# Attention with one low part of k for two heads, reciprocals as 64-column blocks, and split-weight memory in three tiles

## The chip, the cores and the metric

The kernel runs on one core of a Trainium2 chip. The metric is the device time of one execution in microseconds, the median of several runs. The profile is one further execution taken by the hardware profiler. Five engines work from queues of their own: TensorE (PE; its weight loads are shown as PEld), VectorE (DVE), ScalarE (ACT), GpSimd (POOL) and SyncE (SP), which here only issues DMA transfers. Each queue is worked off in order, and an instruction waits at its queue's head until its semaphores are there.

## The reference

Three steps follow one another: attention with pooled queries, a squared-ReLU MLP and an expert layer in which each token goes to one expert.

```python
q_pool = q.reshape(B, H, S // 2, 2, D).mean(axis=3)             # B, H, S, D = 2, 8, 1152, 64
scores = np.matmul(q_pool, k.transpose(0, 1, 3, 2)) / np.sqrt(D)
attn = np.exp(scores - scores.max(-1, keepdims=True))
attn = attn / (attn.sum(-1, keepdims=True) + 1e-09)
x = np.matmul(attn, v)                                          # then (B * S/2, H * D) = (1152, 512)
h = np.maximum(x @ w_in, 0.0)                                   # 512 -> 2048 -> 512
x = (h * h) @ w_out
# top-1 experts: softmax of x @ w_gate, argmax, at most `capacity` tokens per expert,
# out[i] = gate[i] * (relu(x[i] @ w1[e]) @ w2[e]),  8 experts, 512 -> 1024 -> 512
```

## The kernel before, in words

**Attention** works on 8 pairs of heads (a batch and two heads each). A pair has 9 tiles of 128 query rows: for each head four full tiles, and one tail tile in which the 64 last rows of both heads stand together. `tiles` (line 253) lists them: after the first pair always head 0 and head 1 of one row block in turn. For accuracy each fp32 operand of a score is split into a high part that the fast fp32r matmul takes exactly and a low rest. `kqs` holds k and q of a head twice, in partitions 0 to 63 and 64 to 127. `q_piece` (296) has ACT scale the high part of q, `q_low` (301) has DVE put the low part of q into the lower half of the same tile `qT`, and POOL copy the tail's columns into `qzs`. `k_piece` (313) makes, in thirds of 384 columns, the high part of k (line 318 on ACT or 320 on POOL) and its low part `kl` (321, POOL except in the first pair), each head in a set of its own, `kts`; there are four sets, for two pairs of heads. In `s_unit` (326) a third of a full tile's scores takes two matmuls: `qT` with the high k (337, this gives high times high and low times high at once) and `qT` with `kl` (339), whose second half is zero. The tail's third takes four, two per head.

A step of the loop (`run_step`, 432) is, in order: score thirds 0 and 1 of tile n, a transposition group of an older tile (`t_unit`, 363), what a burst held up, third 2, the maximum (`s_max`, DVE, 344), another transposition group, the exponential (`s_exp`, ACT, 349, which also sums), the copy of the first group (380), then, in some steps, a burst; then the extras, the middle transposition group with its copy on DVE (379), and `s_rec` (354): the reciprocal of tile n-1's sums, one column. Scores lie in two sets of PSUM banks that alternate; the third transposition group of an older tile uses the rest of the same banks. The middle group (`TG`, 361) has blocks 4 to 6 of the exponentials and, as fourth, the reciprocal broadcast to 128 columns, so that a transposition puts it along the free axis. A `burst` (383) multiplies the transposed blocks of four tiles with v: 18 matmuls per head pair on PE, then DVE multiplies each head's half with its reciprocal (403, two operations), ACT makes the high part `xh` (407) and POOL the low part `xl` (408). The second burst of a pair, in the next pair's fourth step, is followed by one for the tail. `at(n, ...)` hangs extras on steps; the calls around line 507 hang the preparation of pair p+1 on the steps of pair p: for the second head the sum of q at step 5 of the pair (from 0), piece 0 of k and `q_piece` at 6, `q_low` and piece 1 at 7, piece 2 at 8; in the first pair all one step later.

**Memory of the split weights.** One fp32r tile `ar` (78) holds `xh` and `xl`, and behind them a region that is used twice: in attention for `kts` and `qzs`, then for 16 slots of 1024 columns, which the ring `slots` (192) gives to the high and low halves of the MLP weights, and for the halves of g. `split_hi` and `split_lo` (195, 203) fill two slots, `drop` (213) gives them back. The expert stage takes the whole tile anew as `ar2` (920), so that its loads wait until all of it has fallen free.

**MLP** (`g1`, 751, and `g2`, 776): 48 items of 384 tokens by 128 hidden columns; `mat(n, f, front)` hangs work on item n, before or behind its `g2`. Expert weights, 64 units of 512 KB, are loaded through SP's queue (`load_experts`, 742) into whatever `stage` has free, two thirds through the MLP into another tile, `af`.

**Experts.** Routing of the last tokens, three scatters of token rows by POOL (`scatter`, 557), then `load_disp` (954) reads the rows of each expert back; it waits for the scatters. The first 64 rows of expert 0 come by matmuls (`gather`, 693) instead. `run_batch` (1150) goes through experts 0 to 3, then `rest` (1097) through what they have beyond 64 rows, then 4 to 7.

```python
for o in range(room[0], R0 + RW - UW + 1, UW):     # line 1120
    stage.give(ar2[:, o : o + UW])
load_experts(4)
for e in range(NDT):
    load_disp(e, (0,))
load_experts()
```

Of the kernel before, what the change touches and what calls it, by code (L numbers as in the profile page):

```python
# [9 lines left out]
F32 = mybir.dt.float32  # L10
# [11 lines left out]
def tile_pooled_attention__relu2_mlp__top1_experts(  # L22
# [54 lines left out]
    RW = max(NSET * SETW + 4 * P, NSLOTB * UW + 2 * GB * TB)  # L77
    ar = keep.tile([P, R0 + RW], F32R, name="ar", tag="ar")
# [12 lines left out]
    xh = ar[:, :XN].rearrange("p (a n) -> p a n", a=NPAIR)  # L91
    xl = ar[:, XN : 2 * XN].rearrange("p (a n) -> p a n", a=NPAIR)
# [99 lines left out]
    slots = Ring([ar[:, R0 + i % NSLOTB * UW : R0 + (i % NSLOTB + 1) * UW] for i in range(NSLOTB - 4, 2 * NSLOTB - 4)])  # L192
# [28 lines left out]
    NSET = 4  # L221
# [4 lines left out]
    def kt_set(i):  # L226
        o = R0 + i * SETW
        return ar[:, o : o + S], ar[:, o + S : o + 2 * S], ar[:, o + 2 * S : o + SETW]

    kts = [kt_set(i) for i in range(NSET)]  # L230
    qzs = [
        ar[:, R0 + NSET * SETW + i * 2 * P : R0 + NSET * SETW + (i + 1) * 2 * P].rearrange("p (h n) -> p h n", h=2)
        for i in range(2)
    ]
# [30 lines left out]
    def bufs_of(p, h):  # L265
        return kts[p % 2 * 2 + h]

# [28 lines left out]
    def q_piece(p, h, c=slice(0, SQ)):  # L296
        qT = bufs_of(p, h)[2]
        src = kqs[h][:, S : S + SQ][:, c]
        nc.scalar.activation(out=qT[:, c], in_=src, func=AF.Copy, scale=QSCALE)

    def q_low(p, h, c=slice(0, SQ)):
        qT = bufs_of(p, h)[2]
# [10 lines left out]
    def k_piece(p, h, i, eng=None, hi=None):  # L313
        kh, kl, _ = bufs_of(p, h)
# [6 lines left out]
        (eng or (nc.gpsimd if p else nc.vector)).tensor_tensor(out=kl[:D, c], in0=src[:D], in1=kh[:D, c].bitcast(F32), op=ALU.subtract)  # L321
# [4 lines left out]
    def s_unit(n, i):  # L326
# [4 lines left out]
        c = slice(KS * i, KS * (i + 1))  # L331
        if h is None:
            ops = [(h, qzs[p % 2][:, h, :]) for h in range(2)]
        else:
            ops = [(h, bufs_of(p, h)[2][:, j * P : (j + 1) * P])]
        for m, (h, lhs) in enumerate(ops):
            nc.tensor.matmul(ps, lhsT=lhs, rhs=bufs_of(p, h)[0][:, c], start=(m == 0), stop=False)  # L337
        for m, (h, lhs) in enumerate(ops):
            nc.tensor.matmul(ps, lhsT=lhs, rhs=bufs_of(p, h)[1][:, c], start=False, stop=(m == len(ops) - 1))  # L339


    def s_max(n):
        nm = st[n]["nm"] = sm.tile([P, 1], F32, tag="nm", name="nm", bufs=4)
        nc.vector.tensor_reduce(out=nm, in_=st[n]["S"][:, :, :KS], axis=AX.XY, op=ALU.max, negate=True)  # L344

    def s_exp(n):
        pr = st[n]["P"] = prs[n % NPB]
        su = st[n]["sum"] = sm.tile([P, 1], F32, tag="su", name="su", bufs=4)
# [4 lines left out]

    def s_rec(n):
        su = st[n]["sum"]
        rc = st[n]["rc"] = sm.tile([P, 1], F32, tag="rc", name="rc", bufs=4)
        nc.vector.tensor_scalar(out=su, in0=su, scalar1=1e-9, scalar2=None, op0=ALU.add)
        nc.vector.reciprocal(out=rc, in_=su)


    TG = (range(4), (4, 5, 6, None), (7, 8))

    def t_unit(n, i):
# [4 lines left out]
        else:  # L368
            src = bank_sets[(n + LAG[2]) % 2][:, :2, KS:]
        for m, c in enumerate(TG[i]):  # L370
            x = st[n]["rc"].to_broadcast([P, P]) if c is None else st[n]["P"][:, c * P : (c + 1) * P]
            nc.tensor.transpose(src[:, m, :], x, ident)  # L372
        blocks = slice(4 * i, 4 * i + len(TG[i]))
# [9 lines left out]
    def burst(p, u):  # L383
# [102 lines left out]
    for i in range(NSET):  # L486
        (nc.vector if i == 0 else nc.gpsimd).memset(kts[i][1][D:].bitcast(F32), 0.0)
    for z in qzs:
        nc.gpsimd.memset(z.bitcast(F32), 0.0)
# [17 lines left out]
    for p in range(NPR - 1):  # L507
        n0 = NT9 * p
        for h in range(2):
# [5 lines left out]
            for i in (1, 2):  # L515
                at(m + 1 + i, lambda p=p, h=h, i=i: k_piece(p + 1, h, i, hi=nc.gpsimd))
# [8 lines left out]
    for w in range(5):  # L525
# [5 lines left out]
        n = (when[3 * w + 2] + 2, 0, 64, 67, N + 1)[w] or when[3 * w + 2] + 2  # L531
# [17 lines left out]
    ghs = Turn([ar[:, R0 + NSLOTB * UW + i * TB : R0 + NSLOTB * UW + (i + 1) * TB] for i in range(GB)])  # L549
    gls = Turn([ar[:, R0 + NSLOTB * UW + (GB + i) * TB : R0 + NSLOTB * UW + (GB + i + 1) * TB] for i in range(GB)])  # L550
# [290 lines left out]
    mat(PB + 2 * FH + 1, make_sel)  # L841
    for tb in range(NTB - 1):
# [19 lines left out]
    for n in range(NI):  # L862
# [5 lines left out]
        for f in mtodo.pop((n, 2), []):  # L868
            f()
# [16 lines left out]
    g2(*items[-1], (2,))  # L886
    logits_b(lt + 0, lb[0])
# [32 lines left out]
    ar2 = keep.tile([P, R0 + RW], F32, name="ar2", tag="ar")  # L920
# [199 lines left out]
    for o in range(room[0], R0 + RW - UW + 1, UW):  # L1120
        stage.give(ar2[:, o : o + UW])
    load_experts(4)
# [106 lines left out]
```

## Time and profile before

| | us |
|---|---|
| median of 3 runs (lowest to highest) | 644.79 (644.01 to 646.36) |
| profiled execution, its own time | 646.28 |
| its span, first to last instruction | 644.6 |
| PE busy, weight loads busy | 602.3, 465.2 |
| DVE, ACT, POOL busy | 356.3, 257.2, 162.6 |

Durations below are those of the profiled execution. An engine's busy time is the time in which at least one of its instructions runs. A PE instruction is pipelined: its own duration is longer than the distance to the next one. A timeline row has the start, the duration, the engine, the line of the kernel, the operation, what it writes and reads (in the program's tile names) and how many equal ones were merged; in brackets stands the engine's idle time before it and what ended it. A row that groups instructions has their count, the busy time, the mean duration of one in ns, and the idle time before them.

### The profile page before, as it was taken

Reading aid. Unit: us, or ns where it says so; the run is one execution under the profiler, and the core shown is the slowest. Engines: PE = TensorE matmul, PEld = TensorE weight load, DVE = VectorE, ACT = ScalarE, POOL = GpSimd, SP = SyncE. Lnnn points to the kernel's source line nnn. Section 1 sums busy time; section 2 is a strip of 40 time slices with the busy share of each in tenths; the row PEclk is TensorE's granted clock in tenths of the full one; section 3 lists DMA queues with packets and bytes.
Section 4 is the critical chain, followed back from the end, with each engine's and each line's share of the span. In section 5 each row is a group of like instructions: output and inputs, shape, how many; then the busy total and the mean of one; then the engine's idle time right before and its main releaser. Section 6 shows DMA issues by size and latency. Waiting matters only on the chain. (4 is left out here: it accounts for less than half of the span.)

```text
span 644.6 us, 10110 instructions
## 1 busy us (share of the span) xinstructions
PE 602.3 (93%) x3873; PEld 465.2 (72%) x3873; DVE 356.3 (55%) x655; ACT 257.2 (40%) x511; POOL 162.6 (25%) x223
## 2 busy tenths in 40 slices
PE   5889999999999999999999999999999798999994
PEld 2667787878787878788999999989888344444342
DVE  4777878787878777758467894233545010201110
ACT  3656666666666666632323233232433111110010
POOL 3152636181616263210001330001002301000011
PEclk9999999999999999999999999999999989999998
DMA  8496683353353301303133387001000696399900
GB/s 215 113 317 198 191 255 93 111 140 92 94 156 95 105 36 39 130 13 118 54 104 117 122 293 294 1 0 39 3 2 18 224 397 175 105 393 353 310 9 13
DMA packets 35994, 89.23 MB, mean 138 GB/s; under 512 B 4257, under 2 KB 5157, under 8 KB 35936
## 3 DMA queue, kind: packets, MB, share of 16 engines
q1 hardware_dynamic: 34240, 85.07, 41.9%
q0 software_dynamic: 1376, 2.81, 1.2%
q8 instruction: 35, 0.57, 0.4%
q10 hardware_dynamic: 320, 0.59, 0.3%
q14 instruction: 23, 0.19, 0.1%
HBM read 78.55 MB, written 11.37 MB: 139 GB/s over the span
## 5 line engine op out<-in xcount | busy, mean ns | idle before, releaser
L759 PE MATMUL bs<-ar 128*128 128x384 f32 x576 | 109.0, 338 | 0.0
L759 PEld LDWEIGHTS bs<-ar 128*128 128x128 f32 x576 | 101.7, 188 | 4.7 <-issue 1.2
L344 DVE TENSOR_REDUCE nm<-sc 128x1 f32<-128x1152 f32 x72 | 97.5, 1354 | 10.1 <-PE sc L339 9.0
L337 PE MATMUL sc<-ar 128*128 128x384 f32 x240 | 91.5, 397 | 12.0 <-ACT ar L318 5.4
L349 ACT ACTIVATE af<-sc,nm 128x1152 f32<-128x1152 f32 x72 | 88.0, 1222 | 31.8 <-DVE nm L344 30.3
L785 PE MATMUL bt<-ar 128*128 128x512 f32 x360 | 93.0, 395 | 1.2 <-DVE ar L771 1.2
L339 PE MATMUL sc<-ar 128*128 128x384 f32 x240 | 79.4, 347 | 0.6 <-POOL ar L321 0.6
L785 PEld LDWEIGHTS bt<-ar 128*128 128x128 f32 x360 | 66.4, 188 | 13.8 <-DVE ar L771 1.6
L765 ACT ACTIVATE af<-bs 128x384 f32<-128x384 f32 x48 | 23.6, 491 | 121.6 <-PE bs L759 112.3
L769 DVE TENSOR_TENSOR af<-af 128x384 f32<-128x384 f32 x48 | 28.4, 591 | 72.3 <-ACT af L765 72.3
L397 PE MATMUL ba<-af 128*64 128x256 f32 x576 | 65.7, 382 | 0.6 <-DVE af L379 0.6
L337 PEld LDWEIGHTS sc<-ar 128*128 128x128 f32 x240 | 45.3, 194 | 22.6 <-ACT ar L318 8.5
L379 DVE COPY af<-ba 128x512 f32<-128x512 f32 x72 | 49.3, 685 | 14.5 <-PE ba L372 14.3
L397 PEld LDWEIGHTS ba<-af 128*64 128x64 f32 x576 | 39.9, 137 | 21.8 <-issue 2.3
L380 ACT ACTIVATE af<-bm 128x512 f32<-128x512 f32 x72 | 43.0, 597 | 25.5 <-PE bm L372 25.5
L339 PEld LDWEIGHTS sc<-ar 128*128 128x128 f32 x240 | 46.3, 194 | 2.0 <-POOL ar L321 1.1
L408 POOL TENSOR_TENSOR ar<-af,ar 128x256 fp32r<-128x256 f32 (+1 forms) x24 | 13.9, 593 | 125.8 <-ACT ar L407 125.8
L372 PE MATMUL bm<-ident,af 128*128 128x128 f32 x288 | 43.7, 275 | 0.7 <-ACT af L380 0.6
L201 POOL TENSOR_SCALAR ar<-af 128x1024 fp32r<-128x1024 f32 x15 | 21.2, 1414 | 89.2 <-DVE af L175 54.7
L321 POOL TENSOR_TENSOR ar<-af,ar 64x384 fp32r<-64x384 f32 x42 | 41.9, 998 | 3.5
L372 PE MATMUL ba<-ident,af 128*128 128x128 f32 x216 | 36.6, 278 | 4.6 <-DVE af L379 4.3
L372 PEld LDWEIGHTS bm<-ident,af 128*128 128x128 f32 x288 | 36.1, 142 | 3.8 <-ACT af L380 1.4
(186 smaller groups left out, 799.8 us busy)
## 6 DMA issues: line engine op xcount, KB each, us to landing
af<-in_moe_w_dram SPq DMA_DIRECT2D x32, 512.0 KB, 8.7
ar<-in_moe_w_dram SPq DMA_DIRECT2D x32, 512.0 KB, 9.9
af<-in_q_dram SPq DMA_DIRECT2D x30, 288.0 KB, 3.6
af<-in_k_dram SPq DMA_DIRECT2D x29, 288.0 KB, 5.6
af<-in_moe_w_in_dram SPq DMA_DIRECT2D x8, 1024.0 KB, 6.7
af<-in_moe_w_out_dram SPq DMA_DIRECT2D x8, 1024.0 KB, 4.9
disp<-af SPq DMA_DIRECT2D x6, 771.0 KB
af<-in_v_dram SPq DMA_DIRECT2D x8, 576.0 KB, 4.5
```

What stands on the lines that cost most here:

```text
L321: (eng or (nc.gpsimd if p else nc.vector)).tensor_tensor(out=kl[:D, c], in0=src[:D], in1=kh[:D, c].bitcast(F32), op=ALU.subtract)
L337: nc.tensor.matmul(ps, lhsT=lhs, rhs=bufs_of(p, h)[0][:, c], start=(m == 0), stop=False)
L339: nc.tensor.matmul(ps, lhsT=lhs, rhs=bufs_of(p, h)[1][:, c], start=False, stop=(m == len(ops) - 1))
L344: nc.vector.tensor_reduce(out=nm, in_=st[n]["S"][:, :, :KS], axis=AX.XY, op=ALU.max, negate=True)
L349: nc.scalar.activation(out=pr.rearrange("p (i s) -> p i s", i=3), in_=st[n]["S"][:, :, :KS], func=AF.Exp, bias=st[n]["nm"], accum_out=su,)
L372: nc.tensor.transpose(src[:, m, :], x, ident)
L379: return lambda: nc.vector.tensor_copy(out=dst, in_=src)
L380: return lambda: nc.scalar.activation(out=dst, in_=src, func=AF.Copy)
L397: nc.tensor.matmul(wide(av[hrows[h]]), lhsT=vs[:, h, c * D : (c + 1) * D], rhs=of(c + (c >= RB), h), start=(c == 0), stop=(c == NKC - 1),)
L759: nc.tensor.matmul(ph[:, :TB], lhsT=w[:, cw], rhs=x[:, d, tb * TB : (tb + 1) * TB], start=(n == 0), stop=(n == 3 * NDC - 1),)
L769: nc.vector.tensor_tensor(out=g, in0=r, in1=r, op=ALU.mult)
L785: nc.tensor.matmul(accs[tb][t], lhsT=g[:, ct], rhs=w[:, cw], start=(f == 0 and n == 0), stop=(f == FH - 1 and n == 2),)
```

## The change

The low part of k of both heads now lies in one tile, head 0 in partitions 0 to 63, head 1 in 64 to 127. Each head gets a second scaled copy of q, `q2s`, that is zero in the other head's partitions; the low matmul takes it instead of `qT`. A tail third takes three matmuls, since `qz2` with the shared `kl` serves both heads. `s_rec` writes the reciprocal 64 times, head 0 in the left half and head 1 in the right half of a block; only head 1's tile (and the tail) transposes it, and a full burst needs one multiplication. The region behind `xh` and `xl` becomes three tiles of 6, 6 and 4 slots; the first two hold a pair's k and q in attention. `regrow(i)` takes tile i anew for expert weights: the first at MLP item 46, the second after the last `g2`, the third where the expert weights were loaded before. The rows of experts are read before those, expert 1 first. The fifth split runs at step 72 instead of 73.

```diff
+    GROUPS = (6, 6, 4)
+    ax = keep.tile([P, R0 + 2 * GB * TB], F32R, name="ax", tag="ax")
+    gr_ = [keep.tile([P, n * UW], F32R, name=f"gs{i}", tag=f"gs{i}") for i, n in enumerate(GROUPS)]
...
+    slots = Ring([v for i in (2, 0, 1) for v in cut(gr_[i])])
...
     def q_piece(p, h, c=slice(0, SQ)):
...
-        nc.scalar.activation(out=qT[:, c], in_=src, func=AF.Copy, scale=QSCALE)
+        own = halves_of[h]
+        nc.scalar.activation(out=qts[h][:, c], in_=src, func=AF.Copy, scale=QSCALE)
+        nc.scalar.activation(out=q2s[h][own, c], in_=src[own], func=AF.Copy, scale=QSCALE)
...
         if c.stop == SQ:
-            nc.gpsimd.tensor_scalar(
-                out=qzs[p % 2][:, h, h * D : h * D + TAIL], in0=qT[:, NF * P :].bitcast(F32),
-                scalar1=1.0, scalar2=0.0, op0=ALU.mult, op1=ALU.add,
-            )
+            for o, x in ((qz[:, h, hc], qT[:, NF * P :]), (qz2[own, hc], q2s[h][own, NF * P :])):
+                nc.gpsimd.tensor_scalar(
+                    out=o, in0=x.bitcast(F32), scalar1=1.0, scalar2=0.0, op0=ALU.mult, op1=ALU.add
+                )
...
-        (eng or (nc.gpsimd if p else nc.vector)).tensor_tensor(out=kl[:D, c], in0=src[:D], in1=kh[:D, c].bitcast(F32), op=ALU.subtract)
+        (nc.gpsimd if p else nc.vector).tensor_tensor(
+            out=kl[own, c], in0=src[own], in1=kh[own, c].bitcast(F32), op=ALU.subtract
+        )
...
         if h is None:
-            ops = [(h, qzs[p % 2][:, h, :]) for h in range(2)]
+            ops = [(qz[:, h, :], khs[h]) for h in range(2)] + [(qz2, kl)]
         else:
-            ops = [(h, bufs_of(p, h)[2][:, j * P : (j + 1) * P])]
-        for m, (h, lhs) in enumerate(ops):
-            nc.tensor.matmul(ps, lhsT=lhs, rhs=bufs_of(p, h)[0][:, c], start=(m == 0), stop=False)
-        for m, (h, lhs) in enumerate(ops):
-            nc.tensor.matmul(ps, lhsT=lhs, rhs=bufs_of(p, h)[1][:, c], start=False, stop=(m == len(ops) - 1))
+            jc = slice(j * P, (j + 1) * P)
+            ops = [(qts[h][:, jc], khs[h]), (q2s[h][:, jc], kl)]
+        for m, (lhs, rhs) in enumerate(ops):
+            nc.tensor.matmul(ps, lhsT=lhs, rhs=rhs[:, c], start=(m == 0), stop=(m == len(ops) - 1))
...
     def s_rec(n):
...
-        rc = st[n]["rc"] = sm.tile([P, 1], F32, tag="rc", name="rc", bufs=4)
+        if h is None:
+            rc = st[n]["rc"] = sm.tile([P, 1], F32, tag="rt", name="rt")
+        else:
+            if h == 0:
+                rcs[z] = sm.tile([P, P], F32, tag="rc", name="rc")
+            st[n]["rc"] = rcs[z]
+            rc = rcs[z][:, h * D : (h + 1) * D]
         nc.vector.tensor_scalar(out=su, in0=su, scalar1=1e-9, scalar2=None, op0=ALU.add)
-        nc.vector.reciprocal(out=rc, in_=su)
+        nc.vector.reciprocal(out=rc, in_=su.to_broadcast(rc.shape))
-    TG = (range(4), (4, 5, 6, None), (7, 8))
+    TG = (range(4), (4, 5, 6), (7, 8))
...
+        if i == 1 and h != 0:
+            nc.tensor.transpose(src[:, nb, :], st[n]["rc"].to_broadcast([P, P]), ident)
+            nb += 1
...
-        for h in range(2):
-            nc.vector.tensor_tensor(
-                out=wide(x[hrows[h]]), in0=wide(av[hrows[h]]), in1=of(RB, h, hrows[h]), op=ALU.mult
-            )
+        if u < 2:
+            nc.vector.tensor_tensor(out=wide(x), in0=wide(av), in1=of(RB, 1), op=ALU.mult)
+        for h in range(2 if u == 2 else 0):
+            nc.vector.tensor_tensor(out=x[hrows[h]], in0=av[hrows[h]], in1=of(RB, h, hrows[h]), op=ALU.mult)
...
-                at(m + 1 + i, lambda p=p, h=h, i=i: k_piece(p + 1, h, i, hi=nc.gpsimd))
+                at(min(m + 1 + i, n0 + NT9 - 1), lambda p=p, h=h, i=i: k_piece(p + 1, h, i, hi=nc.gpsimd))
...
-        n = (when[3 * w + 2] + 2, 0, 64, 67, N + 1)[w] or when[3 * w + 2] + 2
+        n = (when[3 * w + 2] + 2, 0, 64, 67, 72)[w] or when[3 * w + 2] + 2
...
+    def regrow(i):
+        t = keep.tile([P, GROUPS[i] * UW], F32, name=f"gf{i}", tag=f"gs{i}")
+        for v in cut(t):
+            stage.give(v)
+        load_experts()
+
+    mat(2 * PB - 2, lambda: regrow(0), 3)
...
     g2(*items[-1], (2,))
+    regrow(1)
...
-    for o in range(room[0], R0 + RW - UW + 1, UW):
-        stage.give(ar2[:, o : o + UW])
-    load_experts(4)
-    for e in range(NDT):
+    for e in (1, 0, *range(2, NDT)):
         load_disp(e, (0,))
-    load_experts()
+    for v in cut(ar2[:, room[0] :]):
+        stage.give(v)
+    regrow(2)
```

## Rows read from the trace of the kernel before

**Rows 1.** Busy time by stage (length, then each engine's busy time, granted clock, DMA).

```profile
0.00:275.00 275.00, 254.22 (x2000) 208.46 (x2000) 206.88 (x373) 172.47 (x334) 118.97 (x162) 1.00 0.49 140
275.00:497.00 222.00, 220.32 (x1220) 196.87 (x1221) 127.11 (x218) 67.09 (x135) 24.91 (x26) 1.00 0.24 85
```

**Rows 2.** Timeline, one tile between two bursts, sixth pair: PE, DVE, ACT.

```profile
177.17 0.41 PE L337 MATMUL sc<-ar 128*128 128x384 f32 x1 [0.20 <-ACT af L380]
...
178.78 1.36 DVE L344 TENSOR_REDUCE nm<-sc 128x1 f32<-128x1152 f32 x1 [0.33 <-PE sc L339]
...
180.18 1.22 ACT L349 ACTIVATE af<-sc,nm 128x1152 f32<-128x1152 f32 x1 [0.43 <-DVE nm L344]
...
181.39 0.37 ACT L380 ACTIVATE af<-sc 128x256 f32<-128x256 f32 x1
```

**Rows 3.** Timeline behind the second burst of a pair: DVE, then PE.

```profile
193.23 0.69 DVE L379 COPY af<-ba 128x512 f32<-128x512 f32 x1
...
194.23 1.34 DVE L344 TENSOR_REDUCE nm<-sc 128x1 f32<-128x1152 f32 x1
...
197.30 0.44 PE L337 MATMUL sc<-ar 128*128 128x384 f32 x1 [0.42 <-ACT af L380]
```

**Rows 4.** Timeline at the border of two pairs: PE in tail and next tile, POOL.

```profile
171.36 0.52 PE L339 MATMUL sc<-ar 128*128 128x384 f32 x2
171.72 0.52 PE L337 MATMUL sc<-ar 128*128 128x384 f32 x2
...
172.51 0.72 POOL L408 TENSOR_TENSOR ar<-af,ar 128x256 fp32r<-128x256 f32 x1 [5.18 <-ACT ar L407]
173.21 0.23 POOL L308 TENSOR_SCALAR ar<-ar 128x64 fp32r<-128x64 f32 x1
...
175.56 1.00 POOL L321 TENSOR_TENSOR ar<-af,ar 64x384 fp32r<-64x384 f32 x1
...
175.76 0.34 PE L339 MATMUL sc<-ar 128*128 128x384 f32 x1
```

**Rows 5.** Timeline, start of the expert stage: SP's loads, PE.

```profile
499.76 1.76 SPq L740 DMA_DIRECT2D ar<-in_moe_w_dram  x4
...
512.49 0.60 PE L971 MATMUL ba<-ident,af 64*128 64x64 f32 x4 [3.31 <-DMA af<-disp]
...
513.57 6.57 PE L994 MATMUL bs<-af,ar 128*64 128x512 f32 x16 [0.47 <-ACT ar L975]
...
521.84 3.65 PE L994 MATMUL bs<-ar 128*64 128x512 f32 x16
```

**Rows 6.** Busy time in two microseconds of that stretch, columns as in rows 1.

```profile
514.00:516.00 2.00, 2.00 (x6) 0.48 (x4) 0.00 (x0) 0.00 (x0) 0.17 (x1) 0.50 0.91 285
```

**Rows 7.** Groups by line and shape: count, busy us, mean ns, idle before.

```profile
L403 DVE TENSOR_TENSOR af<-ba,af 64x256 f32<-64x256 f32 x32 | 13.5, 422 | 26.7 <-PE ba L397 26.2
...
L358 DVE RECIPROCAL rc<-su 128x1 f32<-128x1 f32 x72 | 11.8, 164 | 2.5
...
L299 ACT ACTIVATE ar<-af 128x576 fp32r<-128x576 f32 x15 | 10.1, 675 | 0.9 <-POOL af L294 0.9
...
L372 PEld LDWEIGHTS ba<-ident,rc 128*128 128x128 f32 x72 | 9.8, 136 | 0.7
...
L403 DVE TENSOR_TENSOR af<-bm,af 64x64 f32<-64x64 f32 x16 | 3.6, 223 | 1.5 <-PE bm L397 1.2 <-issue 0.2
...
L713 DVE RECIPROCAL af<-rse 128x3 f32<-128x3 f32 x3 | 0.5, 177 | 0.0
```

**Rows 8.** Timeline at the border of the first two pairs: PE.

```profile
44.99 0.34 PE L339 MATMUL sc<-ar 128*128 128x384 f32 x1
...
48.92 0.45 PE L339 MATMUL sc<-ar 128*128 128x384 f32 x1 [0.63 <-POOL ar L321]
```

**Rows 9.** Line 558's scatters, from issue to landing: from 440 to 490, then from 498 to 505.

```profile
DMA to landing us min/median/max: 2.9/3.3/3.6
...
DMA to landing us min/median/max: 6.3/6.8/7.0
```

More of the change, by code (lines that the diff above doesn't have):

```diff
@@ L76, in tile_pooled_attention__relu2_mlp__top1_experts @@
     NSLOTB = 16
-    RW = max(NSET * SETW + 4 * P, NSLOTB * UW + 2 * GB * TB)
-    ar = keep.tile([P, R0 + RW], F32R, name="ar", tag="ar")
+    GROUPS = (6, 6, 4)
+    ax = keep.tile([P, R0 + 2 * GB * TB], F32R, name="ax", tag="ax")
+    gr_ = [keep.tile([P, n * UW], F32R, name=f"gs{i}", tag=f"gs{i}") for i, n in enumerate(GROUPS)]
+    assert sum(GROUPS) == NSLOTB and 2 * SETW + 2 * P <= 6 * UW
     widths = dict(kq=4 * S, pr=3 * S, pt=6 * (S + P), vs=2 * NKC * D, xr=2 * P + D)
@@ L190, in tile_pooled_attention__relu2_mlp__top1_experts, with cut @@
     nwork = [narrow_ops(kind, g, u == 6) for u, (kind, g) in enumerate(units)]
-    slots = Ring([ar[:, R0 + i % NSLOTB * UW : R0 + (i % NSLOTB + 1) * UW] for i in range(NSLOTB - 4, 2 * NSLOTB - 4)])
+    def cut(t):
+        return [t[:, i * UW : (i + 1) * UW] for i in range(t.shape[-1] // UW)]
+    slots = Ring([v for i in (2, 0, 1) for v in cut(gr_[i])])
     halves = {}
@@ L220, in tile_pooled_attention__relu2_mlp__top1_experts @@
     KS = S // 3
-    NSET = 4
     att = ExitStack()
@@ L224, in tile_pooled_attention__relu2_mlp__top1_experts, with pair_set @@
     bank_sets = [pool.tile([P, 3, 512], F32, name=f"sc{i}") for i in range(2)]
[L226 to L234, printed above, removed]
+    ZW = 3 * P
+    PW = 3 * S + 4 * SQ + ZW
+    def pair_set(i):
+        x = gr_[i][:, :PW]
+        khs = [x[:, h * S : (h + 1) * S] for h in range(2)]
+        kl, q0 = x[:, 2 * S : 3 * S], 3 * S
+        qts = [x[:, q0 + h * SQ : q0 + (h + 1) * SQ] for h in range(2)]
+        q2s = [x[:, q0 + (2 + h) * SQ : q0 + (3 + h) * SQ] for h in range(2)]
+        z = x[:, q0 + 4 * SQ :]
+        return khs, kl, qts, q2s, z[:, : 2 * P].rearrange("p (h n) -> p h n", h=2), z[:, 2 * P :]
+    psets = [pair_set(i) for i in range(2)]
+    halves_of = (slice(0, D), slice(D, 2 * D))
     vs = part("vs", 0, 2 * NKC * D).rearrange("p (h r) -> p h r", h=2)
@@ L347, in s_exp @@
         pr = st[n]["P"] = prs[n % NPB]
-        su = st[n]["sum"] = sm.tile([P, 1], F32, tag="su", name="su", bufs=4)
+        su = st[n]["sum"] = sm.tile([P, 1], F32, tag="su", name="su", bufs=3)
         nc.scalar.activation(
@@ L485, in tile_pooled_attention__relu2_mlp__top1_experts @@
     nc.gpsimd.memset(warm, 0.0)
[L486 to L489, printed above, removed]
+    nc.vector.memset(psets[0][1][D:].bitcast(F32), 0.0)
+    for i in range(2):
+        for h in range(2):
+            (nc.vector if i + h == 0 else nc.gpsimd).memset(psets[i][3][h][halves_of[1 - h]].bitcast(F32), 0.0)
+        for z in psets[i][4:]:
+            nc.gpsimd.memset(z.bitcast(F32), 0.0)
     for _ in range(WARM):
@@ L548, in tile_pooled_attention__relu2_mlp__top1_experts @@
     xts = Turn([af[:, K0 + i * XTW : K0 + (i + 1) * XTW] for i in range(2)])
-    ghs = Turn([ar[:, R0 + NSLOTB * UW + i * TB : R0 + NSLOTB * UW + (i + 1) * TB] for i in range(GB)])
-    gls = Turn([ar[:, R0 + NSLOTB * UW + (GB + i) * TB : R0 + NSLOTB * UW + (GB + i + 1) * TB] for i in range(GB)])
+    ghs = Turn([ax[:, R0 + i * TB : R0 + (i + 1) * TB] for i in range(GB)])
+    gls = Turn([ax[:, R0 + (GB + i) * TB : R0 + (GB + i + 1) * TB] for i in range(GB)])
     hbank = Turn(bank_s)
@@ L867, in tile_pooled_attention__relu2_mlp__top1_experts @@
             g2(*items[n - 2])
-        for f in mtodo.pop((n, 2), []):
-            f()
+        for x in (2, 3):
+            for f in mtodo.pop((n, x), []):
+                f()
     for key in sorted(mtodo):
```

30 lines of the change are left out of this document (17 added, 13 removed).

## The prediction

> **What bounds the kernel now.** I read the windows by stage first, then the timeline of one steady pair of heads, then the waits around the start of the expert stage. The windows [rows 1] show that PE is busy for 254 of the 275 us of attention and for 220.3 of the 222 us of the MLP; DVE, the next, has 207 and 127. In the MLP nothing but PE counts. In attention the busy share misleads, because a ring stands behind it. Call the nine tiles of a pair k0 to k8 (k8 is the tail tile of both heads); the burst (value product) of the first four stands in k7's step, that of the rest in the next pair's k3. In [rows 2] the score matmuls of a tile start at 177.17, DVE takes the maximum at 178.78, ACT the exponential at 180.18 and a copy at 181.39 that ends at 181.76, and only then is the score bank free for the tile two later; the first row says that PE had idled 0.20 for just such a copy. From the start of the maximum to PE's next use of the bank are 3.0 us, whatever PE does meanwhile. Behind a pair's second burst DVE feeds this ring late [rows 3]: the copy at 193.23 and the maximum at 194.23 are one unbroken DVE queue with the sum and reciprocal between them, and PE's tile at 197.30 comes 3.07 after that maximum, with 0.42 idle before it. At the border between two pairs PE runs without a gap [rows 4]: there, work taken from PE is time. In the expert stage PE idles 3.31 us for the rows of expert 1 [rows 5], and then runs 16 matmuls in 6.57 us that take 3.65 us a little later; the granted clock is 0.50 in that stretch, 1.2 instead of 2.4 GHz [rows 6].
>
> **The change part by part.** *Tail tile.* A third of its scores takes 3 matmuls instead of 4. Four matmuls start in 0.72 us, two in 0.36 (171.36 to 171.72 [rows 4]), so 0.18 each, 0.54 per pair. The reciprocal's transpose of one first-head tile in that step goes too: bounded by nothing and by its weight load of 136 ns [rows 7], I take 0.1. PE would reach the last low matmul of the next pair's k0 at 175.76 - 0.64 = 175.12 [rows 4].
>
> *Low k shared by the heads.* The matmul of k0 with kl now reads the rows of both heads, so k0 waits for the second head's three pieces as well. POOL makes the last two of them, and its queue is in order: they stand behind the burst's write-back at 172.51, which waits for ACT, and the last ends at 175.56 + 1.00 = 176.56 [rows 4]. Before, only k1 needed it. The write-back comes earlier by one multiplication of 422 ns [rows 7], and one more copy like that at 173.21 adds 0.23: 176.37. PE therefore idles about 1.3 us in k0 and does its last low matmul 0.6 later than now. Nothing is queued on PE that could pass it: k0's maximum and k1's matmuls stand behind. Between that matmul and k1 lie eight transposes, and k1 used to idle 0.20 there; k1 starts 0.64 later less this idle time, 0.2 to 0.45, I take 0.3; and through the ring so does k3, whose step holds the burst. The 0.54 gained is thus swallowed. Six borders: +1.8. At the first border POOL is later still: k0's last low matmul stands at 44.99, the wait for POOL in k1 ends at 48.92 [rows 8]. After the change k0 waits until about 48.5 (0.42 earlier), and k1 comes a full tile behind, 1.1 later at 49.6. Its maximum follows after 1.61 (177.17 to 178.78 [rows 2]) and k3 after 3.07 more, at 54.3; now the chain from 48.92 with a matmul of 0.45 gives 52.5. That is 1.8. After the last tail no pair follows: -0.5. Sum of the borders: +3.1.
>
> *Reciprocal over 64 columns.* 64 tiles write 64 copies of a reciprocal instead of one. No row shows that. One element takes 164 ns, three take 177 [rows 7], 6.5 ns an element; 63 more make +0.41. From below, an ordinary 64 by 64 operation takes 223, which would be +0.06; below that nothing speaks for a gain, since the output only grows. From above, with 2 ns of scatter on the difference, 7.5 ns an element or +0.47. I take 0.41, the row of the same operation. The Trainium skill ("VectorE: DVE Perf Modes", First, the fixed hardware budget) says that a reciprocal iterates a divide with a repeat count of 8 and gives the clock as 0.96 GHz; worked out from that, an estimate, 63 elements cost 0.53, and the sum below would be 0.9 higher. The rows, at 6.5 ns, come near to it and not to one element per cycle.
>
> First-head tiles copy three blocks instead of four: 128 columns at (422 - 223)/192 = 1.04 ns [rows 7] save 0.13. So behind the second burst the maximum at 194.23 comes 0.41 - 0.13 = 0.28 later, and PE's k7 with it [rows 3]; there the first burst stands, and nothing gives it back. Six pairs: +1.7; the first and the last pair, which have other neighbours there, together +0.5. In k8 to k3 the longer reciprocal lies beside the wait for POOL, in k3 and k7 beside the burst.
>
> *What costs nothing.* The second scaled copy of q on ACT: 16 times up to 0.68 [rows 7]. It is issued behind the second burst and ahead of the first one, where ACT idles; without that cover the ring would be 0.6 longer twice a pair. At the start it holds the first k piece 0.4 at most, and PE waits for the next third of k anyway. One multiplication per burst instead of two saves DVE 16 times 0.42, in the bursts' shade; only what POOL makes of it counts, and it is counted above. The other 31 reciprocal transposes: PE would only wait longer in the ring. The split one step earlier moves POOL work of which no matmul waits. The early loads of expert weights (twelve) go through SP's queue, which issues nothing between the MLP's loads and the expert stage, and run under PE's full MLP.
>
> *Start of the expert stage.* Now four weight loads are issued at 499.76 [rows 5], just as the last three scatters of tokens go out; these land 6.3 to 7.0 us after their issue, where scatters in the quiet MLP took 2.9 to 3.6 [rows 9]. The loads of expert rows wait for the scatters in SP's queue. After the change the weights are in by then and the row loads stand first: 3.4 earlier, against an idle time of 3.31, so PE waits for nothing, and the matmuls behind run at 1.00, as idle times of 0.4 us [rows 3] did not lower the clock of the attention stage [rows 1]: -3.31 and -(6.57 - 3.65) = -2.92 [rows 5, 6]. Together -6.2. What is late next is nothing I can see: later weights are tied to PE's own progress.
>
> **Sum.** Borders +3.1, DVE +2.2, experts -6.2: -0.9. The profiled execution took 646.28 with a span of 644.6, 1.5 above the median of 644.79; it would take 645.4, and carried to the median that is 643.9. Gain and loss almost cancel. A difference under 0.5% (3.2 us) can hardly be told from none.
>
> **The rivals.** *POOL is in time.* If the pieces are there when PE comes, the tail's 0.54 reaches k3 in part: six borders -0.3 each instead of +0.3, the first +0.2 instead of +1.8, together -5.2 more: 638.7. For it: POOL is idle for long stretches; against it: that idling is the in-order wait for the burst [rows 4]. Chance 0.17.
> *The reciprocal is cheap* (+0.06): then 0.07 is saved per pair instead of 0.28 lost: 2.7 less, 641.2. Against it the two rows of the operation. Chance 0.16, of which 0.10 beyond 0.5%. Both together, 636.0: 0.05.
> *Slower: the expert stage gains nothing.* With the change six loads are issued at the end of the MLP; if they still flow when the last scatters go, these land as late as now, the rows of expert 1 are late again and the clock falls. Its point: data of the six must still be moving when the last three scatters go, as that of the four loads from 499.76 on is now [rows 5]. Then +5.3 stays: 650.1. Chance 0.16.
> *Slower: the half clock at the first border.* There PE would do one matmul or two between 45 and 48.5, and after an idle time of 3.31 the clock fell and cost 2.9: so +3, 646.9, or more with a slow reciprocal. The present wait for POOL there, in k1, did not lower it. Chance 0.12, a third of it beyond 0.5%.
>
> **How the numbers follow.** My forecast, 643.9, has 0.34, with a range of its own of 642 to 646 (reciprocal up to 0.47, the border term between 0 and 0.5). Faster: 0.17 + 0.05 + 0.10 = 0.32. Within 0.5%: 0.34 + 0.06 + 0.08 = 0.48. Slower: 0.16 + 0.04 = 0.20. The range from 638.5 to 650.0 takes in the case of POOL in time and the cheap reciprocal, half of the missing expert gain, and leaves out both gains together and the tails.
>
> **What would show it.** Right: a wait of PE's low matmul for POOL at each of the seven borders, near 1.3 us and more at the first; a reciprocal of about 575 ns; the maximum behind the second burst about 0.28 later in its step; no idle of PE for rows of expert 1 and a clock of 1.00 after it; attention longer by about 5 us, the expert stage shorter by about 6. Wrong: no wait for POOL, a reciprocal near 230 ns, or the half clock seen again.

## The result, and the profile after

The change made the kernel slower: a median of 652.49 us (651.7 to 653.45, 4 runs) against 644.82 for the kernel before beside it, a ratio of 1.0116 with an interval of 1.0095 to 1.0137. The forecast was 643.9 with a range from 638.5 to 650.0. The profiled execution of the changed kernel took 653.45, its span is 651.7.

Busy time by stage of the changed kernel, attention and MLP, which answers to [rows 1] with the same columns:

```profile
0.00:286.44 286.44, 253.79 (x1944) 203.66 (x1944) 217.69 (x359) 184.14 (x351) 123.15 (x180) 0.99 0.47 134
286.44:508.44 222.00, 220.31 (x1220) 196.89 (x1221) 126.52 (x217) 67.14 (x135) 24.56 (x26) 1.00 0.31 108
```

PE is busy for as long as before in a longer attention stage (253.8 and 254.2), so what was added is not more work; PE waits longer and, as shown below, works at half clock for a while. The MLP is unchanged. The first MLP matmul starts at 292.01 instead of 280.57, so attention is 11.44 longer; from there to the last instruction, the issue of a scatter that ends at 645.29 (before at 638.46), it takes 353.28 instead of 357.89, 4.61 less.

The waits of PE's score matmuls for POOL's pieces of k (us in total, times, longest):

```profile
PE sc L352 <- POOL gs L332: 11.0, 15, 2.5
```

The regular border of two pairs, timeline of POOL, then of PE; it is the border of [rows 4]:

```profile
181.17 0.78 POOL L434 TENSOR_TENSOR ax<-af,ax 128x256 fp32r<-128x256 f32 x1 [4.79 <-ACT ax L433]
181.93 0.56 POOL L319 TENSOR_SCALAR gs<-gs 128x64 fp32r<-128x64 f32 x2
...
184.86 0.99 POOL L332 TENSOR_TENSOR gs<-af,gs 64x384 fp32r<-64x384 f32 x1
...
184.23 0.44 PE L352 MATMUL sc<-gs 128*128 128x384 f32 x1 [0.43 <-POOL gs L332]
...
185.91 0.45 PE L352 MATMUL sc<-gs 128*128 128x384 f32 x1 [0.84 <-POOL gs L332]
...
186.98 0.94 PE L352 MATMUL sc<-gs 128*128 128x384 f32 x4
```

The wait is there as forecast: PE sits 0.43 and 0.84 in k0 until POOL has the second head's pieces. POOL's chain from the write-back to the end of the last piece takes 185.85 - 181.17 = 4.68; before it was 176.56 - 172.51 = 4.05 [rows 4].

The first border, timeline of PE with k0's and k1's score matmuls (compare [rows 8]) and of POOL with its last piece, and the busy time of six microseconds of it:

```profile
45.91 0.62 PE L352 MATMUL sc<-gs 128*128 128x384 f32 x2 [0.66 <-POOL gs L332]
48.98 0.69 PE L352 MATMUL sc<-gs 128*128 128x384 f32 x1 [2.45 <-POOL gs L332]
...
49.61 0.99 POOL L332 TENSOR_TENSOR gs<-af,gs 64x384 fp32r<-64x384 f32 x1
...
50.66 0.69 PE L352 MATMUL sc<-gs 128*128 128x384 f32 x1 [0.24 <-POOL gs L332]
...
52.70 1.63 PE L352 MATMUL sc<-gs 128*128 128x384 f32 x4
```

```profile
48.00:54.00 6.00, 4.78 (x17) 4.24 (x18) 2.24 (x4) 1.77 (x3) 3.83 (x4) 0.50 0.88 232
```

The granted clock is 0.50 there, 1.2 instead of 2.4 GHz. The trace also records from when to when a clock was granted; by these records it was half from 48.03 to 54.86. Before, it was full at this place.

The reciprocal and the copies beside it, groups by line and shape (count, busy us, mean ns; [rows 7]):

```profile
L380 DVE RECIPROCAL rc<-su 128x64 f32<-128x64 f32 x64 | 35.4, 553 | 2.2
...
L405 DVE COPY af<-ba 128x384 f32<-128x384 f32 x32 | 17.6, 549 | 0.4
```

A reciprocal takes 553 ns instead of 164, and a copy of three blocks 549 ns where one of four took 0.69 us [rows 3].

The start of the expert stage, PE ([rows 5]), and a place 27 us later, where the stage branches to what the experts have beyond 64 rows:

```profile
520.54 0.46 PE L1009 MATMUL ba<-ident,af 64*128 64x64 f32 x4
521.51 3.65 PE L1032 MATMUL bs<-af,ar 128*64 128x512 f32 x16 [0.51 <-ACT ar L1013]
...
547.86 0.43 PE L1120 MATMUL ba<-ident,af 64*128 64x64 f32 x4 [1.32 <-issue]
548.82 5.35 PE L1032 MATMUL bs<-af,ar 128*64 128x512 f32 x16 [0.53 <-ACT ar L1122]
```

The rows of expert 1 are in time and the matmuls behind them take 3.65 instead of 6.57: the whole 6.2 of the forecast. But at 548.82 the same 16 matmuls take 5.35, at half clock (records: 549.79 to 553.20): 1.70 given back. The execution before had the same idle times at this place (1.32 at 542.84, 0.53 at 543.80) and full clock.

Where the 11.44 of attention lies, by how much later each tile's first score matmul starts than before: 1.70 up to the first tail tile; 4.13 from there to k4 of the second pair, over the first border; 0.77 to 0.81 at each of the six regular borders (k8 to the next k4), 4.7 together; 0.21 in each of six stretches from k4 to k8, behind the second burst; 0.19 in the last pair; and 0.54 gained behind the last tail.

### The profile page after: what moved, and what is told of

Same layout as the page of the kernel before. It is cut to its first block, busy times and chain, and to the rows that moved or that the text cites. A ratio compares the mean times of both kernels' runs of the same rounds, so it can differ in the third digit from the quotient of the medians.

```text
span 651.7 us, 10011 instructions
## 1 busy us (share of the span) xinstructions
PE 600.5 (92%) x3817; PEld 460.0 (71%) x3817; DVE 366.5 (56%) x640; ACT 268.9 (41%) x528; POOL 166.5 (26%) x241
## 3 DMA queue, kind: packets, MB, share of 16 engines
q0 software_dynamic: 1376, 2.81, 1.2%
## 5 line engine op out<-in xcount | busy, mean ns | idle before, releaser
L352 PE MATMUL sc<-gs 128*128 128x384 f32 x456 | 124.1, 383 | 23.3 <-POOL gs L332 11.0
L787 PE MATMUL bs<-ax,gs 128*128 128x384 f32 x576 | 109.0, 338 | 0.0
L787 PEld LDWEIGHTS bs<-ax,gs 128*128 128x128 f32 x576 | 101.7, 188 | 4.7 <-issue 1.2
L352 PEld LDWEIGHTS sc<-gs 128*128 128x128 f32 x456 | 77.6, 199 | 38.6 <-POOL gs L332 15.4
L813 PE MATMUL bt<-gs,ax 128*128 128x512 f32 x360 | 93.0, 395 | 1.2 <-DVE ax L799 1.2
L813 PEld LDWEIGHTS bt<-gs,ax 128*128 128x128 f32 x360 | 66.4, 188 | 13.8 <-DVE ax L799 1.6
L405 DVE COPY af<-ba 128x512 f32<-128x512 f32 (+1 forms) x72 | 45.0, 624 | 14.9 <-PE ba L396 14.6
L206 POOL TENSOR_SCALAR gs<-af 128x1024 fp32r<-128x1024 f32 x15 | 20.8, 1390 | 90.0 <-PE bs L787 65.5
L332 POOL TENSOR_TENSOR gs<-af,gs 64x384 fp32r<-64x384 f32 x42 | 41.9, 999 | 3.5
L380 DVE RECIPROCAL rc<-su 128x64 f32<-128x64 f32 x64 | 35.4, 553 | 2.2
```

The lines of the kernel that those rows point to most:

```text
L332: (nc.gpsimd if p else nc.vector).tensor_tensor(out=kl[own, c], in0=src[own], in1=kh[own, c].bitcast(F32), op=ALU.subtract)
L352: nc.tensor.matmul(ps, lhsT=lhs, rhs=rhs[:, c], start=(m == 0), stop=(m == len(ops) - 1))
L380: nc.vector.reciprocal(out=rc, in_=su.to_broadcast(rc.shape))
L405: return lambda: nc.vector.tensor_copy(out=dst, in_=src)
L787: nc.tensor.matmul(ph[:, :TB], lhsT=w[:, cw], rhs=x[:, d, tb * TB : (tb + 1) * TB], start=(n == 0), stop=(n == 3 * NDC - 1),)
L813: nc.tensor.matmul(accs[tb][t], lhsT=g[:, ct], rhs=w[:, cw], start=(f == 0 and n == 0), stop=(f == FH - 1 and n == 2),)
```

## The experiments

My theory after the comparison: shared low k makes PE wait for the end of POOL's queue at every border, the first such wait also lowers the clock, and the wide reciprocal adds a little behind the second bursts. The rivals: the reciprocal on DVE is most of it, or the new memory layout.

**The parts alone.** Three kernels take parts back from the changed one. *Memory alone* has the low k and the reciprocal of before:

```diff
-        khs, kl, qts, q2s, qz, qz2 = psets[p % 2]
...
-            ops = [(qts[h][:, jc], khs[h]), (q2s[h][:, jc], kl)]
+        khs, kls, qts, qz = psets[p % 2]
...
+        ops = [(lhs, khs[h]) for h, lhs in ops] + [(lhs, kls[h]) for h, lhs in ops]
...
-        nc.vector.reciprocal(out=rc, in_=su.to_broadcast(rc.shape))
+        nc.vector.reciprocal(out=rc, in_=su)
```

> Memory in three tiles, early loads and the order of the expert rows alone; attention computes as before. Attention takes 275 in its windows before, and the first MLP matmul starts at 280.57. Theory (shared low k behind POOL's queue, then the wide reciprocal, make attention longer; the memory part only serves the experts): first MLP matmul within 0.5 of 280.6, the rows of expert 1 in time, about -4.6 with a new half-clock stretch and -6.2 without one: 638.6 to 640.2. Rival (the three tiles themselves make attention longer, by other waits or by the start): first MLP matmul near 292, time above 648.

Measured: 640.52, ratio 0.9933 (0.991 to 0.9956). First MLP matmul at 280.93. The memory part leaves attention as it was and is worth some 4.5 by itself; its profile shows the half clock of the branch as well (5.35 for the 16 matmuls). The rival of the memory layout falls.

*Memory and shared low k* takes back the reciprocal alone (last two lines of the diff above, with two multiplications per burst and a transposition per tile):

> The change with the reciprocal as before: one column, transposed for each tile, two multiplications per burst. Theory: the borders stay (six of +0.80, the first of about +4 with the half clock), only some 1.7 of the second bursts goes: attention +9.5 against before, time 650 to 651.5. Rival (the reciprocal on DVE feeds the ring late everywhere and is most of the loss): attention within +3 of before, time near 642.

Measured: 654.47, ratio 1.014 (1.0113 to 1.0167); first MLP matmul at 293.01. Not 1.7 faster than the change but 2.0 slower: the rival falls, and my price for this run was wrong as well. With two multiplications the write-back of the burst stands later, POOL's last piece with it, and PE waits longer at each border: +1.1 to +1.2 instead of +0.8 at five regular ones, and +2.7 at the other, where the clock fell to half as well (219.51 to 222.92) though the two waits, 0.72 and 0.83, were no longer than at the rest. A regular one, PE in k0:

```profile
183.58 0.45 PE L352 MATMUL sc<-gs 128*128 128x384 f32 x1 [0.70 <-POOL gs L332]
...
185.26 0.44 PE L352 MATMUL sc<-gs 128*128 128x384 f32 x1 [0.83 <-POOL gs L332]
```

The second wait is that of the change (0.84), the first is 0.70 instead of 0.43. So beside shared low k the shared reciprocal gains, because it shortens what stands ahead of POOL's queue.

*Memory and wide reciprocal* takes back the low k alone (first four lines of the diff):

> The change with the low k of each head in a tile of its own, the tail with four matmuls, no second copy of q. Theory: no wait for POOL in a tile k0, no half clock at the first border, attention +1.7 against before (0.28 behind each of six second bursts), time 640.5 to 642. Rival (the reciprocal is most of the loss): attention +8 or more, time near 649.

Measured: 641.45, ratio 0.9945 (0.9924 to 0.9966); first MLP matmul at 282.17, 1.24 behind the memory part alone. The reciprocal alone costs about 1, shared low k 11 (beside the wide reciprocal) to 14 (without it). That settles which part it is.

**POOL's order.** The next kernel leaves all parts of the change and moves the second head's pieces of k ahead of the burst's write-back in POOL's queue (`aside` runs ahead of the burst in a step):

```diff
-            at(m + 1, lambda p=p, h=h: k_piece(p + 1, h, 0, hi=nc.gpsimd))
+            piece = lambda p=p, h=h: k_piece(p + 1, h, 0, hi=nc.gpsimd)
+            if m + 1 == n0 + 7:
+                aside.setdefault(m + 1, []).append(piece)
+            else:
+                at(m + 1, piece)
...
-                at(min(m + 1 + i, n0 + NT9 - 1), lambda p=p, h=h, i=i: k_piece(p + 1, h, i, hi=nc.gpsimd))
+                piece = lambda p=p, h=h, i=i: k_piece(p + 1, h, i, hi=nc.gpsimd)
+                if h == 0:
+                    at(m + 1 + i, piece)
+                else:
+                    aside.setdefault(n0 + 7, []).append(piece)
```

> The change with one move: POOL makes the pieces of k of the second head ahead of the first burst's write-back in its queue, in every pair. Same work, other order. Theory: no wait for POOL in k0; a regular border goes from +0.80 to -0.1 or less (the tail's 0.54 now counts in part), the first from about +4 to near 0, at full clock there: attention 9 to 10 shorter than with the change, time 642 to 643.5. Rival (the border is not POOL's order but the ring, with a longer reciprocal in it): POOL's wait goes and another of the same size stands in its place, time within 2 of 652.5.

Measured: 638.01, ratio 0.9894 (0.9873 to 0.9916): 14 below the change and 7 below the kernel before, more than I expected. First MLP matmul at 278.52, 2.05 earlier than before and 13.5 earlier than with the change, where I had expected 9 to 10. POOL's queue at the first border:

```profile
41.69 0.86 POOL L331 TENSOR_SCALAR gs<-af 128x384 fp32r<-128x384 f32 x1
42.63 1.01 POOL L332 TENSOR_TENSOR gs<-af,gs 64x384 fp32r<-64x384 f32 x1
43.72 0.73 POOL L434 TENSOR_TENSOR ax<-af,ax 128x256 fp32r<-128x256 f32 x1
```

The pieces are made while POOL used to wait for the burst, and the write-back, for which nobody waits, comes last. PE waits nowhere for POOL's pieces, a regular border is 0.35 to 0.5 shorter than before (the tail's three matmuls count at last), the first border is 1.05 shorter than before, and the clock's records show no half clock from 24.74 to behind the last matmul.

The same move at the first border alone (`if h == 0 or p:` in the diff above):

> The change with the second head's pieces of k ahead of the write-back in POOL's queue at the first border alone; the six regular borders keep the order of the change. Theory: the wait of 2.45 and the half clock behind it go together, so the first border falls from +4.1 to between -0.5 and 0 and the regular ones stay at +0.80 each, first MLP matmul near 287.5; 4.2 less than the change: 648 to 648.7, or 646.5 if the half clock of the branch in the expert stage is missing too. Rival (half clock and wait are independent): the clock falls at the first border although PE waits for nothing, time above 649.5.

Measured: 645.86, ratio 1.0015 (1.0003 to 1.0026), 6.6 below the change. The first border falls to 1.7 below that of before. In the run before it, with the same instructions up to there, it is 1.05 below; here the step ahead of it had lost 1.4 to a half clock at the first burst (records: 34.17 to 37.58), which the other execution did not have, and part of that seems to come back at the border. No half clock at the border itself, and none at the branch. The six regular borders stand at +0.78 as in the change. The time answers to the 646.5 that I gave for a run without the half clock of the branch; the rival falls.

**What of the reciprocal stays.** Three kernels go on from the run with POOL's new order.

> The run with the second head's pieces ahead, but with the reciprocal as before: one column, a transposition for each tile, two multiplications per burst. Theory: with POOL out of the way the wide reciprocal only costs (0.24 per pair behind the second burst and 0.3 in the first pair), and the earlier write-back no longer counts, so this one is 1 to 2 shorter: 636 to 637. Rival (in the presence of the shared low k the shared reciprocal gains, as the change stood 2.0 below the run without it): 639 to 640.5.

Measured: 637.8, ratio 0.9885 (0.9867 to 0.9903); first MLP matmul at 277.69. Attention is 0.83 shorter than with the shared reciprocal, the time is the same within the intervals. The time lies between my two expectations. With POOL out of the way the shared reciprocal is worth nothing; my 1 to 2 was slightly too much: the old one saves 0.2 per pair behind the second burst, some 1.4 in all, and loses 0.6 of it at the first border (-0.47 against -1.05).

> The memory part and the wide reciprocal with a low k per head, and the second head's pieces ahead of the write-back in POOL's queue. Theory: nothing waits for these pieces there (k1 needs them, and it waited 0.1 to 0.3 at most at the borders), so the order gains under 0.3 a border: 640 to 641.5; what the run with shared low k had below this, about 3, is the tail's fourth matmul (0.54 in each of eight pairs, less the ring). Rival (the order of POOL's queue is worth the same whatever the low k): 638 to 638.5, and the shared low k is worth nothing.

Measured: 640.89, ratio 0.9942 (0.9926 to 0.9958); first MLP matmul at 281.89. The order alone gains nothing where no tile waits for it. So the 3 us between this and the best run are the shared low k, once POOL is in time: the rival of my prediction with 638.7.

The third takes the reciprocal of one column and copies it to 64:

```diff
-        nc.vector.reciprocal(out=rc, in_=su.to_broadcast(rc.shape))
+        nc.vector.reciprocal(out=su, in_=su)
+        nc.vector.tensor_copy(out=rc, in_=su.to_broadcast(rc.shape))
```

> The run with the second head's pieces ahead, and the reciprocal taken of one column and then copied to 64 columns by DVE; still one transposition and one multiplication for two heads. One column takes 164 ns; the copy is bounded by the smallest DVE copies, 150 to 250: 0.31 to 0.41 in place of 0.55. Theory (the reciprocal's length is paid behind the second burst): the 0.24 per pair falls by 0.14 to 0.24 and attention is 1 to 2 shorter: 636 to 637. Rival (a second instruction costs what the shorter one saves): 638 within 0.5.

Measured: 645.97, ratio 1.0013 (1.0002 to 1.0023), 8 slower than without the copy; both theories fall. The step from k7 to k8, with the first burst, grows by 0.81 to 0.91 in five pairs, and by 1.82 in a sixth; in the first pair it grows by 1.59, but there the clock was half (records: 35.20 to 38.62), as in two runs without the copy that lost 1.4 and 1.6 at this place. The timeline ahead of one such burst, DVE and POOL:

```profile
167.84 1.00 POOL L332 TENSOR_TENSOR gs<-af,gs 64x384 fp32r<-64x384 f32 x1
...
168.47 1.80 DVE L381 COPY rc<-su 128x64 f32<-128x64 f32 x1
...
168.80 1.41 POOL L301 TENSOR_TENSOR af<-af 128x576 f32<-128x576 f32 x1
...
170.18 1.34 DVE L357 TENSOR_REDUCE nm<-sc 128x1 f32<-128x1152 f32 x1
...
174.03 0.20 DVE L381 COPY rc<-su 128x64 f32<-128x64 f32 x1
```

The copy takes 0.20 at 174.03, where POOL ends an operation, and 1.80 at 168.47, with POOL at work; it ends within 0.1 of the end of POOL's sum at 170.21. On average the 64 copies took 436 ns: 51 of them 0.2, and the other 13 from 0.29 to 2.81, each of which started during an operation of POOL and ended 0.05 to 0.06 behind the end of one. The next maximum starts right behind it at 170.18, and PE stands behind that. The Trainium skill ("SBUF — State Buffer", SBUF: two separate sides) says that DVE and GpSimd share one pair of ports as an exclusive lock, held for a whole instruction, and names an fp32 copy within SBUF among the DVE operations that take it. By that rule the copy waits for POOL's running operation, and this trace agrees. That a copy waited through two or three operations of POOL in a row, as in six of the 13 cases, the one at 168.47 among them, the rule alone does not tell.

**The size of two terms.** The first kernel takes POOL's two copies of the tail's columns out of the chain, at the change's own order:

```diff
-        if c.stop == SQ:
+        if c.stop == SQ and not (p and h):
+            q_tail(p, h)
...
+            if h:
+                at(n0 + NT9 - 1, lambda p=p, h=h: q_tail(p + 1, h))
```

> The change with POOL's two copies of the second head's tail columns moved behind the pieces of k in its queue, at every border; the pieces still stand behind the write-back. Theory (PE waits for the end of POOL's chain, so what is taken out of the chain comes off the border one for one): the two copies take 0.56 and a gap of 0.1, so a regular border falls from +0.80 to about +0.2; at the first border the copies also waited 0.83 for DVE, so the last piece ends about 1.4 earlier there, 49.2, and the wait of 2.45 shrinks to about 1. Attention 4 to 5.5 shorter than with the change: 646 to 648. Rival (the border is set by the ring and the longer reciprocal, POOL's wait only shows first): borders stay above +0.6, time above 650.

Measured: 645.2, ratio 0.9998 (0.9983 to 1.0013); first MLP matmul at 287.21, 4.8 earlier than with the change, as expected. The time is below my 646 to 648; this profile lacks the half clock of the branch. The same regular border, POOL, then PE:

```profile
178.32 0.78 POOL L440 TENSOR_TENSOR ax<-af,ax 128x256 fp32r<-128x256 f32 x1 [4.80 <-ACT ax L439]
...
181.36 0.99 POOL L338 TENSOR_TENSOR gs<-af,gs 64x384 fp32r<-64x384 f32 x1
...
182.40 0.44 PE L358 MATMUL sc<-gs 128*128 128x384 f32 x1 [0.84 <-POOL gs L338]
...
183.47 0.95 PE L358 MATMUL sc<-gs 128*128 128x384 f32 x4
```

POOL's chain is 182.35 - 178.32 = 4.03 instead of 4.68, and from the write-back to k1 it is 5.15 instead of 5.81: 0.65 off the chain, 0.66 off the border, in each of six (+0.14 instead of +0.79). One for one, as the theory has it. At the first border the wait shrank to 1.62 and the border to +2.3, but the clock fell to half there again (records: 48.34 to 55.17):

```profile
47.90 0.44 PE L358 MATMUL sc<-gs 128*128 128x384 f32 x1 [1.62 <-POOL gs L338]
```

The second keeps PE at work at the first border:

```diff
+        for _ in range(14 if (n, i) == (NT9, 1) else 0):
+            nc.tensor.matmul(ps, lhsT=ops[0][0], rhs=khs[0][:, c], start=True, stop=True)
```

> The change, and at the first border PE repeats the high matmul of the next pair's first tile, second third, 14 times while POOL is late: the same result, the same wait for POOL, but no idle time of 2.45. Theory (the granted clock falls because PE idles there): full clock at the first border, POOL's last piece ends as before at 50.6 and the next tile starts 1.1 behind it instead of 2.1; 1.0 less at the first border, about 651.5, a share of that border's +4.1 of about a quarter. Rival (the clock falls there whatever PE does, or the repeats cost time): 0.5 there again, time 652.5 or more.

Measured: 650.14, ratio 1.0079 (1.0058 to 1.0101); the interval touches that of the change, so the profile has to show it. PE and POOL's last piece there:

```profile
44.92 2.59 PE L352 MATMUL sc<-gs 128*128 128x384 f32 x14
47.35 0.92 PE L354 MATMUL sc<-gs 128*128 128x384 f32 x2
...
48.45 0.99 POOL L332 TENSOR_TENSOR gs<-af,gs 64x384 fp32r<-64x384 f32 x1
...
49.50 0.44 PE L354 MATMUL sc<-gs 128*128 128x384 f32 x1 [0.83 <-POOL gs L332]
...
50.57 0.94 PE L354 MATMUL sc<-gs 128*128 128x384 f32 x4
```

The clock stays full, k1 starts 1.13 behind POOL's last piece (at 49.44) instead of 2.10, and the tiles behind it gain another 1.0. The first border is +1.72 instead of +4.13; 0.45 of the difference lies ahead of it (DVE waits there for an MLP weight, which came later in the change's execution). This is one execution of each kernel, but the other profiles bear it out: at this border the clock fell in the three runs in which PE idled 1.62 or 2.45 (the change, memory and shared low k, and the tail copies last), and in none of the eleven others. So the idle time there lowered the clock, and the half clock cost 2.0, twice what I had written for this run.

**The two halves of the memory part.** Both go on from the best run. In the first the last five weight loads go ahead of the rows of experts:

```diff
-    for e in (1, 0, *range(2, NDT)):
-        load_disp(e, (0,))
     for v in cut(ar2[:, room[0] :]):
         stage.give(v)
     regrow(2)
+    for e in range(NDT):
+        load_disp(e, (0,))
```

> The best run so far (the change with the second head's pieces ahead, 638.0), with twelve weight loads still early, but the last five weight loads ahead of the loads of the expert rows, and the rows in the order of before. Theory (what made the rows late is weight data that moves while the last scatters go out, and the place behind it in SP's queue): rows of expert 1 late again, PE idle 2 to 3.3 there and perhaps the half clock behind it: 640.5 to 644. Rival (twelve early loads alone are what counts): 638 within 0.7.

In the second `regrow(0)` and `regrow(1)` stand beside `regrow(2)`, behind the rows:

> The same best run with the rows first, but no early load: all seventeen weight loads stand behind the loads of the rows. Theory (the early loads only clear the way; without them the weights of expert 1 are issued 5 us later than the four of before were): the rows come in time, then PE waits for weights instead, 1.5 to 4 us, with the half clock possible: 640 to 643. Rival (the order alone is the gain): 638 within 0.7.

Measured: 644.04, ratio 0.9952 (0.9933 to 0.9971), and 642.84, ratio 0.9943 (0.993 to 0.9956). The kernel before took 646.27 beside these two, against 645.0 beside the best run, so that the best run's ratio would give 639.4 here. PE in the first and in the second:

```profile
511.20 0.64 PE L1017 MATMUL ba<-ident,af 64*128 64x64 f32 x4 [3.56 <-DMA af<-disp]
512.32 6.52 PE L1040 MATMUL bs<-af,ar 128*64 128x512 f32 x16 [0.47 <-ACT ar L1021]
```

```profile
523.72 5.35 PE L1038 MATMUL bs<-gf,ar 128*64 128x512 f32 x16 [2.53 <-DMA gf<-in_moe_w_dram]
```

SP's loads of the rows, in the best run and in the first of these:

```profile
503.48 1.73 SPq L1005 DMA_DIRECT2D af<-disp  x3
```

```profile
508.09 1.73 SPq L1005 DMA_DIRECT2D af<-disp  x3
```

With weights ahead the rows are late as before the change (3.31 and 6.57 [rows 5]), half clock included. These loads wait for the scatters: they go out 7.1 behind the issue of the last one, at 500.98, as before (6.8), and in the best run 2.9 behind it, at 500.59. So it is the weights ahead and not the order of the rows, which this run also took back, that makes the first row late. With rows ahead but no early loads, PE waits 2.53 for weights a little later, and the clock falls behind that too (and once more at the branch). Each half taken away costs most of the memory part's 0.7% (0.6 and 0.5); both rivals fall.

## Why the prediction was wrong

*The regular border: right in kind, too small.* The step that failed is "one more copy like that at 173.21 adds 0.23". There are two copies (0.56) with a gap behind them, and the chain grew by 0.63. The last low matmul came 1.1 later instead of 0.6; k1 got back 0.34 of it, as estimated. So +0.79 instead of +0.3, 2.9 over six borders. The write-back itself came 0.38 earlier, as I had it (0.42). The run with the copies behind has +0.14; with the 0.23 that I had counted, one for one, that would be +0.37, so the miss is all but explained by the chain.

*The first border: the rival happened.* Without the half clock the border is +1.72, against my +1.8. With it, +4.13. That 1.72 is so near is in part luck: I had let POOL end 0.42 earlier and counted no copies here, while in the change's execution its chain, from the write-back to the end of the last piece, took 7.04 instead of 6.58, which used up the earlier write-back, and without the half clock's 2.0 the border would have been some 2.1. Even memory alone, with the attention of before, had +0.77 at this border, with DVE waiting for a load there, so single executions do not settle tenths. I had the mechanism as a rival, with a chance of 0.12 and a price of 3; the half clock itself cost 2.0. My argument against, that the present wait of 0.63 had not lowered the clock, compared a short idle time with one of 2.45. The half clock stood behind a wait of 1.62 too.

*The start: taken as nothing.* Up to the first tail tile the change's execution is 1.70 later. In other runs with the same PE work up to there it is 0.99 to 1.14 later where the clock stayed full at the first burst, and 2.14 to 2.63 where it fell. About 1 seems to belong to the change, but which part of it stays open: against memory alone, the wide reciprocal alone and shared low k alone each come 1.1 later there, and memory alone, with the attention of before, comes 0.47 earlier than before.

*The wide reciprocal: right in kind, a quarter too much.* 553 ns instead of my 575, and behind the second burst +0.21 instead of +0.28. The sum of attention's DVE terms, +2.2, was rather 1.2, as the run with it alone shows.

*The expert stage: right at its place, given back in part.* The rows come in time, -6.3. But the half clock at the branch takes 1.70, which leaves -4.6. It stands in the profiles of the change and of four experiments, and not in six others with the same expert stage and the same idle times before it (1.32 and 0.53), nor in the kernel before; what decides between them stays open. I had written that nothing was late next; I had not asked where a clock could fall.

The first and last pair had +0.5 in the forecast and got 1.70 + 0.19. These errors, 2.9 + 2.3 + 1.4 + 1.6 - 0.5, make up the 7.7 between the forecast sum of -0.9 and the 6.8 by which the last instruction came later.

*The rival of POOL in time,* 638.7, was what the change could have been: the run with the pieces ahead gave 638.0. My argument against it for the change as it stood, the in-order wait for the burst, was the right one. The near match is not one of the parts: there a regular border gave -0.5 instead of -0.3, the first -1.05 instead of +0.2, and the start was 1.0 later.

## What to carry to other kernels

When one operand becomes shared, look at when the last producer of any of its halves is done, not at when the first user's own half is, and put the producers ahead of whatever waits in their in-order queue. What stands in such a chain counts one for one, each small copy with its gap. Every new idle time of PE of this size is to be priced twice, once as idle and once, with a chance, at half clock behind it.

## What the runs showed that was not expected

A DVE copy of 64 columns within SBUF took 0.20 or up to 2.81 according to what POOL did, so that replacing a 0.55 reciprocal by 0.16 and such a copy cost 8 us in the whole. Two parts that each cost time (shared low k +14, wide reciprocal +1) cost 12 together, since one shortened the queue that the other waits for. The half clock came behind idle times of 1.62, 2.45, 2.53 and 3.56 us in these runs, but not behind one of 1.77 (it ends at 139.28 in the run with the copied reciprocal, whose records have full clock from 38.62 to 543.79), and at two places (the first burst and the branch) it came and went between executions of the same instructions. So the length of one idle time alone does not tell.
